# The down projection of one chunk in Strassen's form, in a fused transformer block

## Chip, cores, metric

The kernel runs on one core of one Trainium2 chip. The metric is device microseconds of an execution; a kernel's time is the median of its runs. Before the change it is 786.24 us (three runs, 785.5 to 786.73).

TensorE does the matmuls, VectorE and ScalarE work elementwise and empty PSUM banks (the memory that matmuls add their results into), GpSimd helps with sums. All four run at once and wait for one another by semaphores. VectorE, ScalarE and GpSimd are called the helpers below.

## What is computed

One transformer block on 2048 tokens, in bfloat16 with D = 1024 and F = 3584. Cut to what matters here:

```python
h  = x + attention(layernorm(x), wqkv) @ wo          # local, dilated attention, 32 heads
n  = layernorm(h)
h2 = h + ((n @ w_gate) * (n @ w_up)) @ w_down         # [.., 1024] -> [.., 3584] -> [.., 1024]
```

The kernel treats the tokens in four chunks of 512. Chunks 0 and 1 go through gate/up and down projection one after the other; chunks 2 and 3 go through both together.

## The kernel before

Chunks 2 and 3 already use Strassen's form: the two factors of a product are cut into 2 by 2 blocks, and seven block products in place of eight, of sums and differences of blocks, give the result. The sums are work for VectorE, ScalarE and GpSimd. Values are scaled by a power of two and turned to float16 first, so that the sums keep their digits. The gate/up products of chunks 2 and 3, in 14 steps of 256 columns each, are called the pairs below; the down projection behind them is the last stage.

Chunk 1's down projection, the one that the change rewrites, is a plain product in two halves of 512 columns:

```python
def ffn2(c, hf, hT, hs, between={}):
    acc = [psum.tile([128, 512], F32, tag="mm", ...) for t in range(4)]
    for b in range(4):
        for j in range(7):
            for t in range(4):                      # 28 steps x 4 row blocks = 112 matmuls
                nc.tensor.matmul(acc[t][:], lhsT=hT[f][:, bass.ts(t, 128)], rhs=wts["wd", c, hf, b][:, j, :], ...)
    ...
# order of the stage, cut
hT = ffn1(1, lnT2)                                  # gate/up of chunk 1
l2, hs2 = wo_ln2(2)                                 # output projection + layernorm, chunk 2
ffn2(1, 0, hT, hs)                                  # down projection of chunk 1, first half
l3, hs3 = wo_ln2(3)                                 # output projection + layernorm, chunk 3
activation_sums(l2, l3)
ffn2(1, 1, hT, hs, {0: first_sums})                 # second half; in it the first pair's weight sums
```

```python
def weight_sums(n):                                 # for one pair: scale, then four sums per matrix
    nc.vector.tensor_scalar(wt[:], raw[:], scale_gu.s, None, ALU.mult)
    for i in range(2):
        nc.gpsimd.tensor_tensor(sw[:, i, 0], a21, a22, ALU.add)
        ...                                         # three more on GpSimd
```

## Time and profile before

| | before |
|---|---|
| time, median of three runs | 786.24 us |
| span of the profiled run, granted TensorE clock | 785.8 us, 0.997 |
| TensorE busy | 774.1 us, 99% |
| VectorE / ScalarE busy | 583.6 us, 74% / 402.9 us, 51% |
| stage of the change, first matmul behind gate/up to first pair | 449.52 to 525.93: 76.41 us |
| pairs, first pair to first matmul of the last stage | 525.93 to 695.14: 169.21 us |
| last stage, to the end of the span | 90.66 us |

The last three rows are read from TensorE's timeline, where a line's start is exact. The start of a run does not count there: the stage begins between 446.9 and 449.5 us in the profiles of this document. The profiled run of before took 787.53 us, more than any of the three timed runs.

### The profile page before, as it was taken

How to read it: one execution, taken by the hardware profiler on the slowest of the kernel's cores; microseconds unless marked ns; L12 is line 12 of the kernel's file. 1: busy time of each engine (PE TensorE's matmuls, PEld its weight loads, DVE VectorE, ACT ScalarE, POOL GpSimd, SP SyncE). 2: the span in 40 equal slices, each digit the busy share in tenths (PEclk: the TensorE clock that was granted, in tenths of full speed). 3: DMA queues.
4: the chain of work that ended last, by engine and by line, in shares of the span. 5: the costliest groups of instructions: out<-in, count | busy, mean ns of one | idle time of the engine just before them, and what ended most of it. 6: DMA issues, size and time to landing. Idle time of an engine off the chain costs nothing.

```text
span 785.8 us, 10287 instructions
## 1 busy us (share of the span) xinstructions
PE 774.1 (99%) x3670; PEld 359.2 (46%) x3732; DVE 583.6 (74%) x727; ACT 402.9 (51%) x919; POOL 150.9 (19%) x160
## 2 busy tenths in 40 slices
PE   8999999999999999999999999999999999999998
PEld 6544444444444444444444444444444444444444
DVE  5619999999899998999979971733443444579862
ACT  3626534323476652965656610116677777749240
POOL 0000000010000200002000020058678687600000
PEclk9999999999999999999999999999999999999999
DMA  7999594895965878867556489433332423730001
GB/s 248 269 197 243 150 286 98 244 311 127 337 203 170 260 243 234 277 197 264 198 161 208 139 202 328 101 100 102 107 90 72 108 62 100 257 118 28 1 27 54
DMA packets 183683, 135.94 MB, mean 173 GB/s; under 512 B 79056, under 2 KB 176464, under 8 KB 181584
## 3 DMA queue, kind: packets, MB, share of 16 engines
q1 hardware_dynamic: 180048, 113.27, 51.0%
q0 software_dynamic: 3584, 22.02, 8.1%
q8 instruction: 29, 0.48, 0.3%
q14 instruction: 22, 0.18, 0.1%
HBM read 106.95 MB, written 22.02 MB: 164 GB/s over the span
## 4 chain that ended last, share of the span: by engine, by line
PE 74%; DVE 20%; issue 2%; SPq 1%; DMA 1%; ACT 0%; DVEq 0%
PE pu L386 12%; PE acc L605 12%; PE pg L386 12%; PE pz L658 6%; PE py L658 6%; PE px L658 6%; PE wo L507 5%; DVE prod L426 4%; PE ps L386 3%; PE pv L658 3%; PE dx L837 3%; PE dy L837 3%; DVE pv L469 2%; DVE prod L428 2%; SPq L223 1%
## 5 line engine op out<-in xcount | busy, mean ns | idle before, releaser
L386 PE MATMUL ps<-lnT,w_qkv 128*128 128x512 bf16 x721 | 159.0, 379 | 0.8
L386 PEld LDWEIGHTS <-w_qkv 128*128 128x128 bf16 x736 | 71.9, 98 | 86.0 <-issue 0.3
L386 PE MATMUL pu<-lnT,w_wu 128*128 128x512 bf16 x438 | 105.1, 379 | 0.6
L386 PE MATMUL pg<-lnT,w_wg 128*128 128x512 bf16 x440 | 105.1, 379 | 0.4
L605 PE MATMUL acc<-w_wd,gs 128*128 128x512 bf16 x438 | 96.7, 379 | 0.5
L300 ACT CAST sg<-ps 128x512 bf16<-128x512 f32 x96 | 54.8, 590 | 52.7 <-PE ps L386 48.9
L469 DVE TENSOR_TENSOR pv<-vD,at 128x4096 bf16<-128x4096 bf16 x32 | 72.5, 2286 | 0.3
L426 DVE TENSOR_TENSOR prod<-qD,kD 128x4096 bf16<-128x4096 bf16 x32 | 72.4, 2284 | 0.1
L658 PEld LDWEIGHTS <-sw 128*128 128x128 f16 x448 | 43.8, 98 | 52.9
L386 PEld LDWEIGHTS <-w_wg 128*128 128x128 bf16 x448 | 43.8, 98 | 52.8
L605 PEld LDWEIGHTS <-gs 128*128 128x128 bf16 x448 | 43.8, 98 | 52.9
L386 PEld LDWEIGHTS <-w_wu 128*128 128x128 bf16 x448 | 43.8, 98 | 52.9
L179 ACT ACTIVATE rs<-mv,eps 128x1 f32<-128x1 f32 x32 | 9.5, 297 | 101.2 <-DVE mv L176 98.2
L585 ACT CAST us<-pu 128x512 bf16<-128x512 f32 x56 | 33.1, 591 | 50.4 <-PE pu L386 49.3
L507 PE MATMUL wo<-w_wo,oT 128*128 128x512 bf16 x251 | 55.6, 379 | 0.3
L658 PE MATMUL px<-lnT,ws 128*128 128x512 bf16 x211 | 52.6, 379 | 0.6
L658 PEld LDWEIGHTS <-ws 128*128 128x128 f16 x336 | 32.9, 98 | 39.6
L481 POOL DMA_DIRECT2D od<-oD x4 | 2.2, 544 | 249.3 <-DVE oD L479 162.5
L637 POOL TENSOR_TENSOR sw<-ws 128x512 f16<-128x512 f16 x28 | 32.3, 1154 | 87.8 <-PE acc L605 47.2
L580 ACT CAST gs<-pg 128x512 bf16<-128x512 f32 x56 | 33.1, 591 | 12.8 <-PE pg L386 8.7
L507 PEld LDWEIGHTS <-oT 128*128 128x128 bf16 x256 | 25.0, 98 | 30.2
L428 DVE TENSOR_TENSOR prod<-prod 128x4096 bf16<-128x4096 bf16 x16 | 36.6, 2288 | 0.3
(244 smaller groups left out, 1196.6 us busy)
## 6 DMA issues: line engine op xcount, KB each, us to landing
w_wg<-in_B_w_gate_dram SPq DMA_DIRECT2D x14, 1024.0 KB, 6.7
w_wu<-in_B_w_up_dram SPq DMA_DIRECT2D x14, 1024.0 KB, 5.6
w_wd<-in_B_w_down_dram SPq DMA_DIRECT2D x16, 896.0 KB, 8.1
w_wo<-in_A_wo_dram SPq DMA_DIRECT2D x8, 1024.0 KB, 7.4
w_pair<-in_B_w_gate_dram SPq DMA_DIRECT2D x14, 512.0 KB, 4.0
w_pair<-in_B_w_up_dram SPq DMA_DIRECT2D x14, 512.0 KB, 5.3
w_qkv<-in_A_wqkv_dram SPq DMA_DIRECT2D x5, 1024.0 KB, 9.7
kd<-sg SPq DMA_DIRECT2D x32, 144.0 KB, 2.8
```

The lines of the kernel that those rows point to most:

```text
L300: nc.scalar.copy(sg[:, HB:HB + TC], ps[:])
L386: nc.tensor.matmul(ps[:], lhsT=wt[:, ko, bass.ts(j, 128)], rhs=rhs[:, ko, :], start=(ko == 0), stop=(ko == KO - 1))
L426: nc.vector.tensor_tensor(prod[:, j], qD[:], kD[:, :, o:o + SUB], ALU.mult)
L428: nc.vector.tensor_tensor(prod[:, :, 0:16], prod[:, :, 0:16], prod[:, :, 16:32], ALU.add)
L469: nc.vector.tensor_tensor(pv[:, j], vD[:, :, o:o + SUB], at[:, w, None, :].to_broadcast((128, DH, SUB)), ALU.mult)
L507: nc.tensor.matmul(ps[:], lhsT=oTs[c][:, kk, t, :], rhs=wts["wo", c, hf][:, kk, :], start=(kk == 0), stop=(kk == KO - 1))
L580: nc.scalar.copy(gs[:], pg[:])
L585: nc.scalar.copy(us[:], pu[:])
L605: nc.tensor.matmul(acc[t][:], lhsT=hT[f][:, bass.ts(t, 128)], rhs=wts["wd", c, hf, b][:, j, :], start=(f == 0), stop=(f == NF - 1))
L637: nc.gpsimd.tensor_tensor(sw[:, i, 0], a21, a22, ALU.add)
L658: nc.tensor.matmul(ps[:], lhsT=lhs[:, ko, :], rhs=rhs[:, ko, :], start=(fresh and ko == 0), stop=(ko == 3), skip_group_check=not fresh)
L837: nc.tensor.matmul(ps[:, bass.ds(lo, n)], lhsT=lhs[k][:, bass.ts(q, 128)], rhs=rhs[k][:, bass.ds(lo, n)], start=(fresh and k == 0), stop=( ...
```

## The change

The intent is to take away an eighth of chunk 1's down projection matmuls (28 of 224), by the form that chunks 2 and 3 use. The rows of chunk 1 are cut into two halves of 256, the columns into two halves of 512, and F into its even and odd blocks of 128. A product then has two row blocks (`q`) by 14 steps of a 512-wide matmul. S1 to S4 below are the sums and differences of activation blocks, T1 to T4 those of weight blocks. The seven products are spread around the output projections of chunks 2 and 3, to give the helpers time for the sums. The core of the diff, cut:

```diff
-    nc.vector.tensor_scalar(wt[:], raw[:], scale_gu.s, None, ALU.mult)
+    if n == 0:                                     # first pair: weights scaled on ScalarE
+        nc.scalar.activation(wt[:], raw[:], ACTF.Copy, scale=scale_gu.s)
+    else:
+        nc.vector.tensor_scalar(wt[:], raw[:], scale_gu.s, None, ALU.mult)
 ...
-    l2, hs2 = wo_ln2(2)
-    ffn2(1, 0, hT, hs)
-    l3, hs3 = wo_ln2(3)
-    activation_sums(l2, l3)
-    ffn2(1, 1, hT, hs, {0: first_sums})
+    for q in range(2):
+        dprod(ex[q], q, E1["11"], fcells(dn["11"]), True)              # product 1
+    wo_adds(2, {... scales, block conversions, T1, S1 ...})
+    for q in range(2):
+        dprod(ex[q], q, E1["12"], fcells(dn["21"]), False)             # product 2
+        result(1, hs1[q], q, 0, ex[q], scale_d.inv, None)
+    for q in range(2):
+        ev = psum.tile([128, TC], F32, tag="mm", name=f"ev{q}")         # own banks
+        dprod(ev, q, S1, fcells([dn["kx"], dn["vx"]]), True)            # product 3
+        nc.scalar.activation(p5t[:, q, :], ev[:], ACTF.Copy, scale=dn["inv"])
+    t2_half(0); t2_half(1); s3(0, 14)
+    wo_adds(3, {... S2, T3, statistics of chunks 2 and 3 ...})
+    for q in range(2):
+        dprod(ey[q], q, EF["11"], fcells(dn["11"]), False)              # product 4
+        nc.scalar.copy(ex[q][:], ey[q][:])
+        ln_rows(2, 2 + q, l2)
+    ... S4, statistics of chunk 3 ...
+    for t in range(4):
+        ln_rows(3, t, l3)                                               # normalise rows on ScalarE
+    sub([dn["kx"], dn["vx"]], dn["21"], dn["11"])                       # T4
+    weight_sums(0, nc.vector)                                           # first pair's weight sums
+    for q in range(2):
+        dprod(ex[q], q, EF["21"], fcells(dn["12"]), False)              # product 5
+        nc.vector.tensor_tensor(et[:], p5t[:, q, :], hs1[2 + q][:, 512:1024], ALU.add)
+        result(1, hs1[2 + q], 2 + q, 1, ex[q], dn["inv"], et)
+    activation_sums(l2, l3, dn["px"])
+    for q in range(2):
+        dprod(ey[q], q, EF["12"], fcells(dn["22"]), False)              # product 6
+        nc.vector.tensor_tensor(p5t[:, q, :], p5t[:, q, :], hs1[q][:, 512:1024], ALU.add)
+        result(1, hs1[q], q, 1, ey[q], dn["inv"], p5t[:, q, :])
+    for q in range(2):
+        dprod(ex[q], q, EF["22"], fcells([dn["kx"], dn["vx"]]), False)  # product 7
+        result(1, hs1[2 + q], 2 + q, 0, ex[q], dn["inv"], None)
 ...
-    conv_down(down["b21"])
+    conv_down(down["b21"], nc.scalar)               # in the last stage
 ...
-    for i in range(11):                             # warm-up matmuls at the start
+    for i in range(13):
```

Four details named in the change's summary: the weight sums stand ahead of other VectorE work, products 6 and 7 have changed places, product 3 has banks `ev` of its own, and products 5 and 7 add to the same banks `ex`, so that product 7 must wait until VectorE has read the result of product 5.

## The prediction

> **What bounds the kernel now.** I read the totals first.
>
> ```profile
> PE 774.1 (99%) x3670; PEld 359.2 (46%) x3732; DVE 583.6 (74%) x727; ACT 402.9 (51%) x919; POOL 150.9 (19%) x160
> ```
>
> TensorE is busy 99% of the 785.8 us, at a granted clock of 0.997, so time leaves only with matmuls. The view of TensorE's waits says how much it stands still:
>
> ```profile
> PE ps L349 <- DMA w_qkv<-in_A_wqkv_dram: 2.1, 2, 1.0
> PE warm_ps L294 <- DVE warm L280: 1.2, 1, 1.2
> PE dy L837 <- DVE dn_t2a L830: 1.0, 1, 1.0
> PE dy L837 <- DVE h L846: 0.6, 1, 0.6
> PE dy L837 <- DVE dn_t2b L830: 0.3, 1, 0.3
> ```
>
> That is 3.3 us at the start and 1.9 us in the last stage; nothing waits in the middle. TensorE's timeline over the stage that changes (start, length, engine, line, what) is solid:
>
> ```profile
> 449.52 13.98 PE L507 MATMUL wo<-w_wo,oT 128*128 128x512 bf16 x63
> 463.34 0.38 PE L544 MATMUL l1psgu<-rowbgu,ones 128*128 128x512 bf16 x1
> 463.55 0.38 PE L544 MATMUL l1psd<-rowbd,ones 128*128 128x512 bf16 x1
> 463.77 24.34 PE L605 MATMUL acc<-w_wd,gs 128*128 128x512 bf16 x110
> 487.94 13.98 PE L507 MATMUL wo<-w_wo,oT 128*128 128x512 bf16 x63
> 501.76 24.34 PE L605 MATMUL acc<-w_wd,gs 128*128 128x512 bf16 x109
> 525.93 1.89 PE L658 MATMUL px<-lnT,ws 128*128 128x512 bf16 x8
> ```
>
> Each half of chunk 1's down projection is 112 matmuls (some records are missing) in 487.94 - 463.77 = 24.17 us: 0.2158 us each. The windows view shows how idle the helpers are in those two stretches (columns: window, length, then PE, PEld, DVE, ACT busy):
>
> ```profile
> 463.80:487.90 24.10, 23.99 (x111) 10.95 (x112) 4.10 (x16) 0.50 (x2) 3.56 (x4) 1.00 1.02 286
> 501.80:525.90 24.10, 23.94 (x110) 10.91 (x112) 8.98 (x11) 0.50 (x2) 9.02 (x8) 1.00 0.45 109
> ```
>
> VectorE works 13 of 48 us and ScalarE 1 of 48. This is the room that the new form wants to fill.
>
> **Unit costs.** The final stage already runs this form for chunks 2 and 3, so its rows give the prices:
>
> ```profile
> 706.67 3.23 DVE L786 TENSOR_SCALAR hq<-hq,sbh 128x512 f16<-128x512 bf16 x12
> 714.02 2.09 DVE L876 TENSOR_TENSOR dn_b11a<-hq,hq 128x512 f16<-128x512 f16 x6
> 730.75 2.01 DVE L830 TENSOR_TENSOR dn_t2a<-dn_b22a,dn_t1a 128x3584 f16<-128x3584 f16 x1
> 708.89 3.78 ACT L784 ACTIVATE hq<-hq,sbh 128x512 f16<-128x512 bf16 x6
> 717.46 3.28 ACT L784 ACTIVATE dn_b22a<-dn_b22a,sbd 128x3584 f16<-128x3584 bf16 x1
> ```
>
> Start to start, a 512-wide VectorE difference takes 0.335 us and a 3584-wide one 1.94; between these two a 256-wide one is 0.20. A 512-wide scaling on VectorE takes 0.26, a 3584-wide one 1.07 (its row starts 1.06 before the next), a 256-wide one about 0.20. On ScalarE a 512-wide scaling takes 0.61, a 3584-wide one 3.17.
>
> **What the Trainium skill says.** "TensorE: Matmul & The Clock Gate", section "Wait — 56ns, not 53.3ns?", gives N / 2.4 GHz + about 2.5 ns for a warm matmul, 215.7 ns at N = 512: the trace has 0.2158 us. "VectorE: DVE Perf Modes", section "Why `tensor_tensor` can't do 2×_2P or 4×", keeps a two-tensor operation at two elements a cycle; the trace agrees, 1.94 us for a 3584-wide difference against 1.07 for a scaling. "ScalarE: Activation LUTs", section "What ACT_TABLE_LOAD costs", has an ACTIVATE at 186 ns + 0.833 ns per column, 93 ns more per pointer operand, and 93 ns overlapped back to back; for 3584 columns and one pointer that is 3.27 us, traced 3.28. From it I estimate 1.13 us for a 1024-wide row normalisation (two pointers) and 3.6 us for the 4096-wide weight scaling, neither of which ScalarE does before. "PSUM — Partial Sum Buffer", section "PSUM bank collisions raise a hardware error", asks for a semaphore per bank: a product into a bank waits until the last reader is done. No run shows a collision; the waits are in the program.
>
> **The change on TensorE.** Seven products of two 128-row blocks by 14 steps are 196 matmuls in place of 224, all still 512 wide: 28 x 0.2158 = 6.04 us less. One added scale total (a matmul) returns 0.22. The two extra warm-up matmuls cost 2 x 0.43 = 0.86 us before the first transposes, but TensorE then waits for the weights until 7.74 and again until 9.85 us, so I count nothing. Without stalls: -5.82 us.
>
> **The change on the helpers.** VectorE gets 2 weight conversions (2.1 us) plus 14 activation scalings (2.8), 8 weight-block differences of 1.94 (15.5), 56 activation differences (11.2), and weight sums for the first pair, four 1024-wide operations at about 0.6 (2.4): 34 us. It loses the LayerNorm of chunk 2 and the normalisation of chunk 3, about 9 us. ScalarE gets about 50 us: four large weight conversions (12.7), scalings (8.6 + 5.6), chunk 2's statistics (8.7), eight row normalisations (9.1), the first pair's scaling (3.6) and copies. All lies beside TensorE as long as the results are ready in time, so I walked the order of the instructions on each engine with these prices, with chunk 1's gate/up stage ending at 449.7 (one more matmul inside).
>
> - Product 1 runs 449.7 to 455.8. Chunk 3's attention, 2.1 us later because of two weight conversions ahead of it, ends at 455.3. The output projection of chunk 2 runs to 470.1, the second product to 476.1.
> - The third product wants S1 and T1 at 476.1. VectorE, full from 456 on, has T1 at 473.4 and S1's first block at 474.3: 1.7 us to spare, if the late block of weights, issued when the attention frees its room at 455.3, has landed by 469.6.
> - The output projection of chunk 3 runs from 482.2 to 496.0; its activations, reloaded from 470.1 on (3.7 us to issue, 6.6 us median to land), are there by about 480.
> - VectorE is then about 3 us behind TensorE: the statistics of chunk 3 end at 502.2, S4 at 505.0, T4 at 509.0. ScalarE normalises chunk 3's four rows from 505.2 to 509.8 and scales the first pair's weights to 513.4. Only then can VectorE do the weight sums (to 516.1), and behind them, in order, the addition and the result that empties the first ex bank: about 517.4.
> - TensorE does the fourth product to 502.0, the fifth to 508.1, the sixth to 514.1. The seventh adds to that same bank and must wait from 514.1 to 517.5: **a stall of 3.4 us**. Then it is 3.0 + 3.0 us to the pairs, which start at 523.5 instead of 525.9.
>
> **The last stage** loses 2 conversions from VectorE (2.1 us) to ScalarE, which idles there. The next results wait for a product that ends no sooner, so only about 0.8 us reaches T2; of the 1.3 us of stalls on T2, about 0.7 go.
>
> **The sum:** 786.2 - 5.8 + 3.4 - 0.7 = 783.1. The slacks of 1 to 2 us in a stage with some 100 instructions behind one another on VectorE, and weights whose landing shares the engines with attention's stores, will not all hold; I add 0.7 us for it, a choice and not a measurement. **783.8 us.**
>
> **Rivals.** (a) Everything is hidden: 786.2 - 5.8 - 0.7 = 779.7. For it: 48 us of nearly idle helpers, and the change has reordered products to give time. Against it: the chain statistics, normalisation, weight scaling, weight sums, result is serial over two engines and lands after 514 by my count. (b) The helpers become the bound: the prices are 10% low over the 50 us in which VectorE is full, which is 5 us straight onto the stall: about 789. For it: no idle time from 456 to 509 by my walk. Against it: the prices are taken from same-shaped rows. (c) A late transfer: the attention's store must land before the last weight block's room is free, and before it other loads of 0.9 to 1 MB queue; DMA share was already 1.02 in 463.8 to 487.9. If the late blocks land 3 us after my 469.6, third product and VectorE both slip: about 787. But the second load of the output weights is gone (2 MB less), which speaks against it. (d) The pair stage: its sums now start later by the shift of VectorE, but GpSimd takes about 9 of the 12.1 us per pair, so it catches up; no change.
>
> **Range and chances.** (a) with a small stall sets the low end, 780.0; (b) or (c) in part the high end, 787.5. For faster by 2% it would need 770.5, more than all removed matmuls: 0.01. Slower by 2% is 802.0, 22 us of stalls: 0.02. Within 2%: 0.97.
>
> **What would show it.** Right: 196 matmuls of the new products in place of 224; a single wait of some 3 us on the result before the seventh product, released by VectorE, with VectorE released by ScalarE's weight scaling before it; T2 stalls under 1 us at the end; pairs starting at about 523 to 524. Wrong: waits before the third product (then a transfer or S1 is to blame), waits on the reloaded attention output before the chunk 3 projection, waits of ScalarE's copies in the fourth product, a longer gate/up stage because ScalarE's added sums delay its evacuations, or pairs slowed by their weight sums.

## The result

| | before | after |
|---|---|---|
| time, median (lowest to highest) | 785.87 us (785.27 to 786.73), 4 runs | 783.80 us (781.72 to 784.65), 4 runs |
| ratio after to before, 95% interval | | 0.9969 [0.9947, 0.9991] |
| span and clock of the profiled run | 785.8 us, 0.997 | 779.9 us, 0.999 |
| stage of the change | 76.41 us | 73.71 us |
| pairs | 169.21 us | 169.53 us |
| last stage | 90.66 us | 89.77 us |

A ratio is the mean time of one kernel's fast runs over that of the other's of the same rounds, so not quite the ratio of the medians. By the 2% measure the kernels are the same; the gain is about 2 us. The spans of the two profiles differ by 5.9 us, but 2.6 us of that lie ahead of the stage (449.52 against 446.89), at the start of the run.

The page of the changed kernel has this line of totals:

```profile
PE 766.8 (98%) x3648; PEld 355.0 (46%) x3707; DVE 614.9 (79%) x805; ACT 473.5 (61%) x1028; POOL 142.4 (18%) x152
```

TensorE has fewer matmuls and works 7.3 us less, VectorE 31 us more and ScalarE 71 us more. (The 28 added absolute sums for the scale of chunk 1's products, some 0.8 us each, are 23 us of ScalarE's share; nearly all lie in gate/up.) The view of TensorE's waits, with the line, what it waited for, and the us in total, times and longest us:

```profile
PE ex L787 <- DVE h L792: 3.2, 1, 3.2
PE dy L787 <- DVE h L792: 0.6, 1, 0.6
PE dy L787 <- DVE prodx L780: 0.3, 1, 0.3
```

The first line is new: one wait of 3.2 us in the middle, on a result (`h`) that VectorE reads out of the `ex` bank. The two lines on `dn_t2a` and `dn_t2b` of before, 1.3 us together, have become the third one, 0.3 us. TensorE's timeline of the stage (start, length, engine, line, what; a wait in brackets) shows where the new wait lies:

```profile
446.89 6.21 PE L787 MATMUL ex<-w_dn,gs 128*128 128x512 f16 x28
...
509.70 1.67 PE L787 MATMUL ey<-lx,gs 128*128 128x512 f16 x7
514.56 1.67 PE L787 MATMUL ex<-kx,gs 128*128 128x512 f16 x7 [3.18 <-DVE h L792]
...
520.60 1.89 PE L680 MATMUL px<-lnT,ws 128*128 128x512 bf16 x7
```

No line between the first and the second shown has a bracket: six products and two output projections follow one another without a wait. The wait is before product 7. What VectorE and ScalarE did up to it, from their timelines:

```profile
503.96 2.02 DVE L780 TENSOR_TENSOR vx<-w_dn,w_dn 128x3584 f16<-128x3584 f16 x1
510.42 0.69 DVE L661 TENSOR_TENSOR sw<-ws 128x1024 f16<-128x1024 f16 x1 [4.44 <-ACT ws L654]
...
512.96 0.68 DVE L978 TENSOR_TENSOR et<-ep,h 128x512 f32<-128x512 f32 x1
513.75 0.75 DVE L792 SCALAR_TENSOR_TENSOR h<-ex,inv_h1d,et 128x512 bf16<-128x512 f32 x1
```

```profile
502.14 4.64 ACT L869 ACTIVATE lnr<-h,lnroom,rs 128x1024 bf16<-128x1024 bf16 x4 [0.67 <-DVE lnroom L969]
506.69 3.69 ACT L654 ACTIVATE ws<-w_pair,sbgu 128x4096 f16<-128x4096 bf16 x1
```

VectorE finishes T4 at 505.98 and then stands idle for 4.44 us. Next in its order is the first weight sum, and that needs the weights that ScalarE scales only at 506.69, behind the normalisation of four rows. Behind the sums come the addition and the result that TensorE waits for. The result itself (the fifth product had ended by 505.3) could have been read out during those idle 4.44 us. By this reading the wait is a matter of order in a queue, not of work; three experiments below test it.

The windows view shows how full the helpers are now (window, length, then PE, PEld, DVE, ACT, POOL busy, clock, DMA share, GB/s), first over the output projection of chunk 3, then over products 4 to 6:

```profile
479.20:493.00 13.80, 13.69 (x64) 6.27 (x64) 13.80 (x39) 11.91 (x23) 0.00 (x0) 1.00 0.02 5
493.00:511.20 18.20, 18.20 (x86) 8.23 (x84) 13.59 (x33) 14.45 (x13) 0.00 (x0) 1.00 1.05 228
```

VectorE is busy in all 13.80 us of the first window; its timeline has no bracket behind 458.75 up to 505.98. In the second window it is 4.6 us short, which is the idle stretch just seen.

One thing in the table does not fit. The profiled run is the fastest of the four: 779.9 us of span at a clock of 0.999. The other three have spans of 782.1 to 782.9 at 0.997 to 0.998. So the profile that came back is not of a typical run. The first experiment looks at another one.

### The profile page after: what moved, and what is told of

Read it like the earlier page. It is cut to its first block, busy times and chain, and to the rows that moved or that the text cites. A ratio compares the mean times of both kernels' runs of the same rounds, so it can differ in the third digit from the quotient of the medians.

```text
span 779.9 us, 10436 instructions
## 1 busy us (share of the span) xinstructions
PE 766.8 (98%) x3648; PEld 355.0 (46%) x3707; DVE 614.9 (79%) x805; ACT 473.5 (61%) x1028; POOL 142.4 (18%) x152
## 4 chain that ended last, share of the span: by engine, by line
PE 88%; DVE 9%; ACT 1%; issue 1%; DMA 1%; SPq 0%; DVEq 0%
PE ps L392 20%; PE pu L392 12%; PE pg L392 12%; PE dx L787 6%; PE pz L680 6%; PE acc L626 6%; PE py L680 6%; PE px L680 6%; PE wo L513 4%; PE pv L680 3%; PE dy L787 3%; DVE h L834 1%; PE ps L355 1%; PE ex L787 1%; DVE prodx L780 1%
## 5 line engine op out<-in xcount | busy, mean ns | idle before, releaser
L626 PE MATMUL acc<-w_wd,gs 128*128 128x512 bf16 x219 | 48.2, 379 | 0.3
L661 POOL TENSOR_TENSOR sw<-ws 128x512 f16<-128x512 f16 x26 | 30.0, 1154 | 87.6 <-PE py L680 80.4
L185 ACT ACTIVATE rs<-mv,eps 128x1 f32<-128x1 f32 (+1 forms) x25 | 7.4, 297 | 50.3 <-DVE mv L182 47.1
L541 ACT ACTIVATE junkd<-w_wd 128x512 bf16<-128x512 bf16 x56 | 34.3, 613 | 0.0
L626 PEld LDWEIGHTS <-gs 128*128 128x128 bf16 x224 | 21.9, 98 | 26.4
L697 ACT COPY py<-px 128x512 f32<-128x512 f32 x28 | 16.0, 570 | 29.6 <-PE px L680 29.6
```

Source lines behind the costliest of these rows:

```text
L541: nc.scalar.activation(junk, src, ACTF.Abs, accum_out=self.l1[:, k:k + 1])
```

## The experiments

Twelve kernels ran, in three batches of four. The kernels of a batch ran on one chip with the kernel before beside them: 785.61, 785.49 and 785.52 us. All gave correct results. In the profile of each, the three stages took:

| kernel | time, us | ratio to before | wait(s) in the stage and the first pair | stage | pairs | last |
|---|---|---|---|---|---|---|
| before, 13 warm-ups | 785.55 | 0.9998 | none | 76.41 | 169.21 | 90.64 |
| changed kernel again | 783.65 | 0.9972 | 3.18 | 75.39 | 169.21 | 89.76 |
| changed, 11 warm-ups | 783.34 | 0.9972 | 3.68 | 75.63 | 169.22 | 89.8 |
| sums behind the result | 779.89 | 0.9926 | 0.22 | 70.37 | 169.81 | 89.78 |
| filler in the wait | 782.31 | 0.9957 | 0.38, 0.15 | 73.71 | 169.53 | 89.77 |
| sums on GpSimd | 783.20 | 0.9966 | 2.30 | 70.36 | 173.36 | 89.79 |
| products 6, 7 not swapped | 790.04 | 1.0059 | 9.23 | 81.47 | 169.21 | 89.77 |
| product 3 in the ex banks | 785.30 | 0.9992 | 1.32, 2.87 | 76.33 | 169.21 | 89.76 |
| scaling on VectorE | 779.20 | 0.9918 | 0.15 | 70.56 | 169.53 | 89.75 |
| b21 on VectorE | 784.25 | 0.9986 | 3.18 | 75.39 | 169.21 | 90.77 |
| sums behind, again | 779.10 | 0.9919 | 0.22 | 70.36 | 169.83 | 89.79 |
| all in order of need | 778.78 | 0.9915 | none | 70.36 | 169.22 | 89.79 |

### The changed kernel again

No edit: the changed kernel, run beside the next three.

> The changed kernel once more, beside the others of this call. Theory: the middle stage gains 2.7 us in every run (6.0 us of matmuls less, 3.2 us of waiting more), the last stage 0.7 to 1, and what is left of the difference between runs (779.9 to 782.9 us of span so far) is the start, which depends on whether TensorE's clock is released during the warm-up matmuls. So times of about 781.5 where the start is fast and about 784 where it is slow, ratio to before about 0.997. Rival: the middle stage itself differs from run to run (late weight blocks); then a second profile shows a wait other than the 3.2 us before the seventh product, or another length of it.

Measured: 783.65 us (782.67 to 783.79, five runs), ratio 0.9972 [0.9959, 0.9984]. The stage took 75.39 us and not 73.71, though its wait was the same 3.18 us. TensorE's timeline of this run:

```profile
515.30 2.88 PE L787 MATMUL ex<-kx,gs 128*128 128x512 f16 x7 [3.18 <-DVE h L792]
517.98 2.19 PE L787 MATMUL ex<-vx,gs 128*128 128x512 f16 x7
```

Seven matmuls take 1.67 us at full speed; behind the wait the first seven took 2.88 and the next seven 2.19. So the theory that the middle stage gains 2.7 us in every run fell: here it gained 1.0 us. The rival was right that the stage varies, but no other or longer wait makes it. The windows view of this run, cut behind the wait (the third figure from the end is the granted clock), says why:

```profile
515.30:517.00 1.70, 1.70 (x5) 0.64 (x5) 1.60 (x3) 0.00 (x0) 0.00 (x0) 0.59 0.23 77
517.00:518.70 1.70, 1.70 (x5) 0.60 (x4) 1.67 (x2) 0.00 (x0) 0.00 (x0) 0.50 0.23 77
```

The granted clock is 0.59 and 0.50 in the first 3.4 us after the wait, and back at 0.91 in the next 1.7. That costs 75.39 - 73.71 = 1.68 us. TensorE counts as busy all that time, so no busy share and no wait shows it. In the same stretch of the first profile the clock was 1.00:

```profile
514.50:516.20 1.70, 1.64 (x8) 0.78 (x8) 1.56 (x4) 0.00 (x0) 0.00 (x0) 1.00 0.23 77
```

The Trainium skill's page "TensorE: Matmul & The Clock Gate", section "What's actually happening", describes the mechanism: the clock is halved after an idle window of about 3.4 us and comes back after a busy one, and the window runs on its own, so that it depends on chance where a wait falls in it. A wait of 3.18 us that costs 1.68 us in one profile and nothing in another agrees with the part of chance, and a slow stretch of about 3.4 us with the way back. The length does not agree: 3.18 us is shorter than the idle window, and waits of 2.30 and 2.87 us below slow the clock too. That idleness is the cause is a theory that this one run does not show; the filler experiment below tests it. No run shows the window itself.

### Eleven warm-up matmuls in the changed kernel

```diff
-    for i in range(13):
+    for i in range(11):
```

> The changed kernel with 11 warm-up matmuls in place of 13. Theory: the start is set by when the clock is released; with 11 the warm-up ends before the first transposes and the released clock is met less often, so the mean is 0.5 to 2 us slower than the changed kernel, and a profile shows the 128x128 products of the start at the long spacing until about 14 us. Rival: the two matmuls change nothing and the fast start of the profile was luck; then the mean lies within 0.5 us of the changed kernel's.

Measured: 783.34 us (782.78 to 784.22), ratio 0.9972 [0.996, 0.9985], the same as with 13. The wait before product 7 was 3.68 us and seven matmuls after it took 3.10 us. The two added warm-ups are not what takes or gives the time.

### Thirteen warm-up matmuls in the kernel before

```diff
-    for i in range(11):
+    for i in range(13):
```

> The kernel before with 13 warm-up matmuls in place of 11, nothing else. Theory that the start belongs to the warm-up: 0.5 to 2 us faster than before, some runs 2.5 us faster. Rival that it is luck: ratio 1.000 within 0.0007.

Measured: 785.55 us (785.27 to 785.73), ratio 0.9998 [0.9985, 1.0012]. Both ways round, the warm-ups do nothing that can be measured here.

### The weight sums behind the fifth product's results

```diff
     sub([dn["kx"], dn["vx"]], dn["21"], dn["11"])
-    weight_sums(0, nc.vector)
     retire(2)
     ...                                            # loop of product 5 with its two results
+    weight_sums(0, nc.vector)
     retire(1)
```

> Only the first pair's weight sums are issued on VectorE after the two results that empty the ex banks, not before them. Theory: the 3.2 us wait is the order on VectorE: the results need only the fifth product (done at 505.2) and TensorE reaches the seventh at 511.4; with the sums behind them the wait is gone and the pairs start 3.2 us earlier; 3 us faster than the changed kernel, ratio to before about 0.993. Rival: the stall moves: the pair stage then waits for the weight sums or for the four activation sums behind them, and 1 to 3 us of the gain come back as waits in the first pair.

Measured: 779.89 us (779.42 to 780.47), ratio 0.9926 [0.9913, 0.9938], clock 1.0. VectorE now goes from T4, which ends at 507.2, through the addition to the result without a gap, and waits for ScalarE only behind it:

```profile
507.94 0.75 DVE L792 SCALAR_TENSOR_TENSOR h<-ex,inv_h1d,et 128x512 bf16<-128x512 f32 x1
...
511.66 0.69 DVE L661 TENSOR_TENSOR sw<-ws 128x1024 f16<-128x1024 f16 x1 [1.39 <-ACT ws L654]
```

The stage takes 70.37 us: 76.41 - 28 x 0.2158 = 70.37, so here the removed matmuls come out of the time in full. No wait and no slow clock is left in it. Against the changed kernel of the same batch that is 3.8 us. With this order the wait is gone, and nothing else was changed; the late scaling on ScalarE turns out below to be as necessary for it. (Pairs took 0.6 us more; see the last experiment.)

### Filler matmuls in the wait

```diff
+    fill = psum.tile([128, TC], F32, tag="mm", name="fill")
+    for k in range(13):                            # nobody reads fill
+        nc.tensor.matmul(fill[:], lhsT=EF["12"][k][:, 0:128], rhs=fcells(dn["22"])[k], start=True, stop=True)
     for q in range(2):
         dprod(ex[q], q, EF["22"], fcells([dn["kx"], dn["vx"]]), False)     # product 7
```

> The changed kernel with 13 unneeded 128x512 matmuls (into a bank that nobody reads) between the sixth and the seventh product, so that TensorE works through 2.8 us of its 3.2 us wait. Theory (the idle wait lets the clock drop, and the matmuls after it run at half rate for some 3 us): what is left of the wait is under 1 us, the first seven matmuls after it take 1.67 us and not 2.9, the pairs start 73.7 us after the stage's start and not 75.4, the mean granted clock is 0.999 or more, and the time is about 1.7 us below the changed kernel's 783.6: 782.0. Rival (the slow matmuls have another cause, such as their freshly written operands): seven matmuls still take over 2.5 us and the time is 783.6 or more.

Measured: 782.31 us (782.03 to 782.97), ratio 0.9957 [0.9944, 0.9969], four of five runs at clock 1.0 and one at 0.999.

```profile
514.86 1.67 PE L787 MATMUL ex<-kx,gs 128*128 128x512 f16 x7 [0.38 <-DVE h L792]
```

The result that TensorE waits for comes as late as ever (67.6 us after the stage's start), but the matmuls behind it run at full speed, and the stage takes 73.71 us like that of the first profile. TensorE does 13 matmuls more and the kernel is faster by about 0.0015 of 785 us, 1.2 us; the changed kernel ran in another batch and the two intervals overlap, so the time alone would not decide. Two things speak for the theory: all five runs have a clock of 0.999 or more, where four of five of the changed kernel have 0.998 or less (a mean in which the start is mixed in), and in the profile the same matmuls, with the same operands, are no longer slow. The first profile, too, had them at full speed. So it is idleness that slows the matmuls, not their operands. What a wait costs here is its length and, in six of the seven profiles with a wait of 2.3 us or more, 1.4 to 1.7 us besides.

### The weight sums on GpSimd

```diff
-    weight_sums(0, nc.vector)
+    weight_sums(0)                                 # on GpSimd, as for all other pairs
```

> The changed kernel with the first pair's weight sums on GpSimd in place of VectorE. Theory (VectorE's place in order, behind the weight sums that wait for ScalarE, makes the stall): the 3.2 us wait on the fifth product's result goes, as it did when the sums were put behind the result; pairs start 70.4 us after the stage's start; GpSimd needs about 4.5 us for the first half of the sums, after 510.4, so the pairs wait for it at most 1 us; time 779.5 to 781. Rival (the fifth product's result is late by the amount of VectorE's work and not by the wait for ScalarE): VectorE saves 2.5 us of work, the stall shrinks to about 0.7 us and does not vanish, same time within 1 us, so the profile's wait before the addition decides: theory none, rival some 0.7 us.

Measured: 783.20 us (782.3 to 783.66), ratio 0.9966 [0.9951, 0.998]. The wait before product 7 was gone and the stage took 70.36 us, as the theory had it. The time, 779.5 to 781 expected, was missed: the pairs took 173.36 us, 4.15 more than before. The first pair waited 2.3 us, and then ran at a low clock. TensorE's timeline, then VectorE's:

```profile
521.54 1.02 PE L680 MATMUL pv<-prodx,sw 128*128 128x512 f16 x4 [2.30 <-DVE h L792]
```

```profile
514.81 2.17 DVE L674 TENSOR_TENSOR prodx<-lnT 128x2048 f16<-128x2048 bf16 x1
...
520.74 0.75 DVE L792 SCALAR_TENSOR_TENSOR h<-ey,inv_h1d,ep 128x512 bf16<-128x512 f32 x1
```

The same activation sums take 1.22 us each in the other kernels. Here they overlap with GpSimd's sums, and both slow down: GpSimd's first sum, before the overlap, takes 1.15 us, the third 2.13. VectorE's four sums began 64.1 us after the stage's start, earlier than the 66.1 of the changed order, and still ended later, at 72.1 against 70.8.

```profile
513.77 2.13 POOL L663 TENSOR_TENSOR sw<-ws 128x512 f16<-128x512 f16 x1
```

The Trainium skill's "GPSIMD Engine Reference", section "1. Specifications", says that GpSimd shares its SBUF interfaces with VectorE and that operations with two SBUF inputs contend; these rows agree. So the sixth product's result comes at 521.49, and the first pair's third bank, which that result empties, is free only then: the wait of 2.30 us ends at 521.54. Its other condition, GpSimd's first four sums, was met at 517.99, 7.4 us after they began and not the 4.5 expected. The sum `4.15 = 2.30 + 1.85` is once more a wait and, but for 0.17 us of hand-over, a clock that fell: the granted clock was 0.73 from 521.0 to 525.0.

### The last two products not swapped

```diff
     activation_sums(l2, l3, dn["px"])
+    for q in range(2):
+        dprod(ex[q], q, EF["22"], fcells([dn["kx"], dn["vx"]]), False)     # product 7 first
+        result(1, hs1[2 + q], 2 + q, 0, ex[q], dn["inv"], None)
     for q in range(2):
         dprod(ey[q], q, EF["12"], fcells(dn["22"]), False)                 # then product 6
         ...
-    for q in range(2):
-        dprod(ex[q], q, EF["22"], ...)
-        result(...)
```

> The changed kernel with its last two products in their old order: the product that adds to the fifth's bank comes straight behind the fifth. Theory (the swap gives the result of the fifth 6.0 us to get done): the wait grows from 3.2 by 6.0 to 9.2 us, and the time from 783.6 to 789.6, up to 790.5 with the slow clock after the wait. Rival (the wait belongs to the operands, not the bank, so the order does not matter): 783.6.

Measured: 790.04 us (789.99 to 791.51), ratio 1.0059 [1.0043, 1.0074].

```profile
515.42 3.15 PE L787 MATMUL ex<-kx,gs 128*128 128x512 f16 x7 [9.23 <-DVE h L792]
```

The wait is 9.23 us, longer by the 6.05 us of the product that no longer stands in between. Without the swap the change would have lost time. The rest of the stage is 81.47 - 70.36 - 9.23 = 1.88 us. The first profile, at full clock, has 73.71 - 70.36 - 3.18 = 0.17 us of hand-over there; the other 1.7 us are the low clock again.

### The third product in the banks of the second

```diff
     for q in range(2):
-        ev = psum.tile([128, TC], F32, tag="mm", name=f"ev{q}")
+        ev = ex[q]
         dprod(ev, q, S1, fcells([dn["kx"], dn["vx"]]), True)
```

> The changed kernel with the third product in the banks of the second instead of two banks of its own. It then waits for the second's results on VectorE, which stand behind the last four sums of S1: about 1.4 us of wait before the third product. Theory (the later stall is set by VectorE's and ScalarE's chain, which does not move): the stall before the seventh product shrinks by the same 1.4 to about 1.8 us[...], so pairs start at 73.7 and the time is 782 to 783.7, not above the changed kernel. Rival (waits add up): 783.6 + 1.4 = 785.0.

Measured: 785.30 us (782.99 to 786.83, six runs), ratio 0.9992 [0.9975, 1.0009].

```profile
476.02 1.67 PE L787 MATMUL ex<-kx,es 128*128 128x512 f16 x7 [1.32 <-DVE h L792]
...
517.03 3.12 PE L787 MATMUL ex<-kx,gs 128*128 128x512 f16 x7 [2.87 <-DVE h L792]
```

My theory fell: I had expected the second wait to shrink by the whole first one. It shrank by 0.31 us only, and the rival's 785.0 is right. The timelines show the mistake. The chain that sets the second wait hangs on TensorE: VectorE is waiting for the output projection of chunk 3 (0.67 us of idle time, released by that projection, at 483.99), so a delay of the projection delays the statistics, the normalisation and the scaling behind it. Against the start of the stage, the weight sums came 1.16 us later than in the changed kernel (512.89 - 448.20 against 510.42 - 446.89). Waits on such a path add up. The banks of its own are worth 1.32 - 0.31 = 1.0 us, and the stage, 76.33 against 75.39, agrees.

This run adds a wait of 2.87 us to those that let the clock fall (3.12 us for seven matmuls), while the wait of 1.32 us did not. One of its six runs was at 782.99 us and clock 0.999, the other five at 785.1 to 786.8 and 0.996 to 0.998; a run in which the clock did not fall would look like that one, but only the profiled run can be looked into.

### The first pair's weights scaled on VectorE

```diff
-        if n == 0:
-            nc.scalar.activation(wt[:], raw[:], ACTF.Copy, scale=scale_gu.s)
-        else:
-            nc.vector.tensor_scalar(wt[:], raw[:], scale_gu.s, None, ALU.mult)
+        nc.vector.tensor_scalar(wt[:], raw[:], scale_gu.s, None, ALU.mult)
```

> The changed kernel with the first pair's weights scaled on VectorE, as the kernel before does it; the order on VectorE is left as it is. Theory (the stall is the time for which VectorE stands idle behind ScalarE's normalisations and its 3.69 us scaling): VectorE goes on at once from 505.9, scaling 1.28 us, four sums 2.5, addition 0.8, result 0.8, so that the result is there some 3.2 us earlier than in the changed kernel; no stall, or at most 0.3 us, pairs start 70.4 to 70.8 us after the stage's start, the clock stays at 1.0, time 779.8 to 780.5. Rival (VectorE's amount of work is the limit, so 1.28 us more of it costs 1.28 us): 784.5 or more, with a stall of 3 us or more.

Measured: 779.20 us (778.61 to 779.42), ratio 0.9918 [0.9904, 0.9931].

```profile
506.75 1.28 DVE L653 TENSOR_SCALAR ws<-w_pair,sbgu 128x4096 f16<-128x4096 bf16 x1
...
511.48 0.75 DVE L789 SCALAR_TENSOR_TENSOR h<-ex,inv_h1d,et 128x512 bf16<-128x512 f32 x1
```

VectorE ends T4 at 506.83, goes straight on to the scaling, has 1.28 us more to do and keeps the order of the changed kernel, and the wait is gone but for 0.2 us between products 6 and 7, which is the stage's 70.56 against 70.36. So it was neither the amount of VectorE's work nor the weight sums as such, but ScalarE's 3.69 us behind the normalisations. The scaling was moved to the engine that was late. Two unlike edits, the changed order and this one, take the wait away, the first wholly, the second but for 0.2 us.

### The b21 conversion back on VectorE

```diff
-    conv_down(down["b21"], nc.scalar)
+    conv_down(down["b21"])
```

> The changed kernel with the last stage's b21 weight conversion put back on VectorE, as in the kernel before. Theory (this move alone makes the 0.9 us gained in the last stage): the waits on the second weight differences return to about 1.3 us from 0.3, the last stage takes 90.6 us in place of 89.8, and the time is 0.9 us above the changed kernel's 783.6: 784.5. Rival (the gain comes from the other moves around the last stage): 783.6 and 89.8 us.

Measured: 784.25 us (783.25 to 785.59), ratio 0.9986 [0.9972, 0.9999]; last stage 90.77 us in place of 89.76.

```profile
PE dy L787 <- DVE prodx L780: 1.3, 2, 1.0
```

The two waits on T2 are back at their 1.3 us. This move alone makes the gain of the last stage: 1.01 us between these two profiles.

### Sums behind the result, and all in the order of need

First the sums behind the fifth product's results again, as the basis (the diff is above), then a version with the rest of VectorE's queue sorted by when TensorE needs it:

```diff
     for q in range(2):
         dprod(ey[q], q, EF["12"], fcells(dn["22"]), False)                 # product 6
         nc.vector.tensor_tensor(p5t[:, q, :], p5t[:, q, :], hs1[q][:, 512:1024], ALU.add)
         result(1, hs1[q], q, 1, ey[q], dn["inv"], p5t[:, q, :])
+        if q == 0:
+            weight_sums(0, nc.vector)
+    sums = activation_sums(l2, l3, dn["px"])       # now a generator: t1 | t2 | t3, t4
     for q in range(2):
+        next(sums)
         dprod(ex[q], q, EF["22"], fcells([dn["kx"], dn["vx"]]), False)     # product 7
         result(1, hs1[2 + q], 2 + q, 0, ex[q], dn["inv"], None)
+    list(sums)
```

> The kernel with the first pair's weight sums behind the fifth product's results, run again as the basis of the next. Every theory: 779.9, no wait before the seventh product, pairs start 70.4 us after the stage's start, 0.2 us of wait in the first pair.

> As the previous kernel, and VectorE's other work there put in the order in which TensorE needs it: the sixth product's first result ahead of the weight sums, its second ahead of the activation sums, the seventh product's two results between the activation sums. Theory (the 0.6 us that the pair stage took longer with the new order is the first pair's products waiting for banks that these results empty): the pair stage goes back from 169.8 to 169.2 us, no wait on results in the first pair, time 0.6 us below the previous kernel: 779.3. Rival (the pair stage's 0.6 us has another cause): 779.9.

Measured: 779.10 us (778.57 to 779.54), ratio 0.9919 [0.9905, 0.9932], and 778.78 us (778.13 to 779.28), ratio 0.9915 [0.9901, 0.9928]. The pairs go from 169.83 back to 169.22 us, and the first pair's wait on a result is gone, which is the theory's mechanism and its 0.6 us. In the time of whole runs the two differ by 0.3 us, which the intervals do not tell apart. The last version beats both kernels: by 0.85% the kernel before, and by about 0.6% the changed one, if its two ratios to the kernel before are set against each other.

## Why the prediction was right

The time was right, 783.8 predicted and measured, and so was the main step. Read against the start of the stage, the walk through the engines' orders held to 0.3 us at every point:

| us after the first matmul behind gate/up | predicted | changed kernel, first profile |
|---|---|---|
| T1 ready (S1 and product 3 follow) | 473.4 - 449.7 = 23.7 | 470.57 - 446.89 = 23.7 |
| T4 ready | 59.3 | 59.1 |
| rows of chunk 3 normalised | 60.1 | 59.9 |
| first pair's weights scaled | 63.7 | 63.5 |
| weight sums done | 66.4 | 66.2 |
| result of product 5 out of the bank | 67.7 | 67.6 |
| pairs start | 73.8 | 73.7, but 75.4 in the second profile |

Point by point:

- **Matmuls, -5.8 us.** Right. The stage without its wait is 6.05 us shorter (four profiles show 70.36 or 70.37), and the scale total moved into gate/up gives one matmul back.
- **The wait, +3.4 us.** Right in place, cause and size: 3.18 us in brackets, and 73.71 - 70.36 = 3.35 us of time with the hand-over. That the cause is the chain from ScalarE's scaling through VectorE's order is shown from two sides, by the changed order and by the scaling on VectorE.
- **The helpers' work.** Right in the stage: between the two first profiles VectorE's busy time there goes from 39.5 to 66.4 us and ScalarE's from 5.6 to 57.3, against +25 and about +50. Of the two ScalarE estimates, a row normalisation took 4.64 / 4 = 1.16 us (1.13 estimated) and the weight scaling 3.69 (3.6 estimated). The 23 us of absolute sums in gate/up were not in the count, but cost no time: chunk 1's gate/up takes 96.90 us in place of 96.69, the one added matmul.
- **The last stage, -0.7 us.** The mechanism is right. The term was undersized: 0.89 us from before to after, and 1.01 us between the two kernels that differ in nothing else.
- **Reserve, +0.7 us for slacks that do not hold.** This step failed. All slacks held. No wait before product 3, none on weights, none on the reloaded activations. What took its place is a loss that the prediction did not know: 1.4 to 1.7 us of low clock after the wait, in six of seven profiles. The prediction had counted a wait by its length alone. The profile of before could have warned only in part: its waits behind the start are 1.02 us and shorter, but at the start the granted clock was 0.50 from 10 to 12 us, just behind the two waits of 1.03 and 1.04 us.
- **Warm-ups count for nothing.** Right, in both kernels.
- **Rivals.** All hidden (779.7): wrong for this kernel, and just what the kernels without the wait measure, 778.8 to 779.9. Helpers as the bound (789): wrong; VectorE is full from 459 to 506 and still in time. Late transfers (787): wrong, no such wait in any profile. Pair stage unchanged: right for the changed kernel to 0.3 us; but it is sensitive, since a later VectorE or GpSimd delays the first pair's banks by 0.6 to 4.2 us.

The sum as measured is -5.8 + 3.35 + 1.7 - 0.9, about -1.7 us, and the runs have 783.65 - 785.61 = -2.0 us; the prediction had -2.4 from its base of 786.24. So the time came out right partly because an unjustified reserve of 0.7 us and a base that was 0.6 to 0.75 us higher than the later runs of the same kernel stood in for a real 1.7 us. That is luck in the number; the mechanism of the wait is not.

What stays open: how often the clock falls after the 3.2 us wait, and why waits of 2.30 and 2.87 us are enough for it. Of seven profiles with a wait of 2.3 us or more, six show it. The mean clock of the other runs (0.996 to 0.999) mixes it with the state of the clock at the start, so they cannot be sorted by it.

## What to carry to other kernels

When a new form removes matmuls, follow each engine's queue in order up to the point where TensorE next needs something: here a single entry, standing ahead of a result that was ready and itself waiting for another engine, took back, by its wait and the low clock, some 5 of the 7 us that the change had to give, and moving it cost one line and 0.6 us in the next stage. Give work to the engine that is idle at that moment, not to the one that is idle on average: ScalarE had the room over the stage, but it was the last to finish at the place that counted. And a wait of some 3 us on TensorE is to be priced with the slow matmuls behind it, which neither the busy share nor the list of waits shows; look at the granted clock in the microseconds after it, and at more than one run.

## What the Trainium skill lacked or had wrong

- "TensorE: Matmul & The Clock Gate": it puts the fall of the clock at an idle window of about 3.4 us. In these runs single waits of 2.30, 2.87 and 3.18 us were enough, and one of 3.18 us in another run of the same kernel was not; a wait of 1.32 us, seen once, was not either. The slow stretch cost 1.4 to 1.7 us each time.
- "GPSIMD Engine Reference" names the contention with VectorE but gives no size for sums like these. Here two-input sums that overlapped went from 1.22 to 2.17 us on VectorE and from 1.15 to 2.13 us on GpSimd.
- "TensorE: Matmul & The Clock Gate", section "Back-to-back issue gap", gives about 131 ns per matmul of N = 512 as what streams with weight loads sustain. The traces have 24.17 us for 112 of them with a weight load each, 215.8 ns, which agrees with the other figure of that page, the one that the prediction used.
